# The second w_in converted during the attention, kept in device memory, and fetched later

## The chip, the cores and the metric

One core of one Trainium2 chip runs the kernel. The metric is the device time of an execution in microseconds, here as the median of three runs. The profile is of one execution.

## The reference, cut to what matters

Inputs come as float64 and are read as pairs of 32-bit words. Three stages follow each other: an attention over 2 batches, 8 heads, 768 rows and 64 columns, in which a query sees only keys of its own cluster; a layer pair with a SiLU; a layer pair with a PReLU. The change touches only how `moe2_w_in`, the first weight of the last pair, is brought in.

```python
def _moe_ref(x, w_in, w_out):
    h = x @ w_in
    g = h * (1.0 / (1.0 + np.exp(-h)))
    return (g @ w_out).astype(np.float32)

def _moe2_ref(x, w_in, w_out, alpha):
    h = x @ w_in
    g = np.maximum(h, 0.0) + alpha * np.minimum(h, 0.0)
    return (g @ w_out).astype(np.float32)

def reference(**kwargs):
    ...
    attn_out = _attn_ref(**attn_kwargs)
    x = np.ascontiguousarray(attn_out.transpose(0, 2, 1, 3)).reshape(B * S, H * D)
    x = _moe_ref(x=x, **moe_kwargs)
    return _moe2_ref(x=x, **moe2_kwargs)
```

Here x has 1536 rows of 512; w_in is 512 x 2048 and w_out 2048 x 512 in both pairs.

## The kernel before, in words

**Number format.** Each fp32 factor is kept as two fp16 parts (hi and lo) with a power of two as scale, and each product is three fp16 matmuls (hi hi, hi lo, lo hi). A weight is handled in eight pieces. A piece of 1 MB comes in as float64 (`load_piece`, L649), is made fp32 on the chip (`to_f32`: L660 on ACT, L664 on ACT or L668 on POOL, L671 and L674 on DVE), its sum of squares is taken (`sum_sq`, L700 on ACT, for the second pair), summed over the partitions by a matmul with ones (`all_sum`, L223 on PE), turned into a scale by small DVE instructions (`pow2_scale`, L172 to L179), and split into the two fp16 parts (`split`). `split` has four modes: in "a" and "d" DVE makes lo (L687, L682), in "b" and "c" POOL does (L693, L697); "c" also scales on POOL (L695) and makes hi on ACT (L696). The strings SPLIT and EXP_ON choose, piece by piece, the mode and the engine of the third step.

**Attention.** It works in units: one head of one tile of 128 queries, 96 units in all, 48 for each batch. A unit computes the scores (L509 and L513 on PE), their negated maximum (L517 on DVE), after every second unit the rows that carry the maxima (`to_rows`, L529 to L541), the scores again in the other orientation (L561, L562), the exponential (L564 on ACT), its hi part (L570 on ACT) and lo part (L571 on DVE), and the product with the values (L586 to L596 on PE). The maxima run two units ahead, the values two units behind. After four units a half of a tile of attention output is scaled and split (`x_done`, L613 to L623), and after eight units it is transposed by a DMA from SyncE's queue (L626).

**Layer 1** (first weight pair) takes the tiles in seven chunks and is interleaved with the attention: 32 steps a chunk, between which `attend` emits units up to UNITS_BY_CHUNK. A chunk has 192 matmuls of the first product (L951, with L959 to L965 on ACT and DVE behind them) and 192 of the second (L984, with L991 behind).

**Layer 2** (second weight pair) runs after that in three blocks of 512 rows: for each of 16 f twelve matmuls (L1056), then L1065 and L1066 on DVE, L1069 on ACT, L1070 on DVE; then the second product (L1087) and the output (L1093, L1095). Its input is split by `split_x2` (L1033 to L1043).

**The second weights.** `w2_start` (L1110) is called when the last unit has been emitted. It loads alpha (L1005, L1008) and hangs the tasks of both second weights into the list `bg`, from which one task is taken per step of layer 1: loads of w_in into three buffers of 8 KB a partition, `conv` and `scale` of its eight pieces, loads of w_out into the same three buffers, `conv` of its eight pieces, and its scale. The eight splits of w_out (`late`) follow in layer 2, two per f. They write into the place (o_w) of w_in of layer 1.

**What sets the order.** The Python order is a priority. A scheduler with a timing model of its own orders each engine's instructions before the run: it moves one ahead where it expects it to be ready. So work of later lines stands between that of earlier ones, and each engine then keeps to its list. DMAs go out from SyncE's list.

**Memory.** One arena holds everything; regions are used again when free. o_kvraw (8 KB a partition) takes raw K and V until the second batch is prepared; o_x2 takes the result of layer 1, its last 8 KB that of the last two chunks; w_in of layer 2 lies at o_a + 24 KB, where the attention has V, Q and o_kvraw.

## Time and profile before

| | |
|---|---|
| median of 3 runs | 877.53 us (876.75 to 878.41) |
| the profiled execution | 876.54 us |
| its span, first to last instruction | 874.6 us |
| mean granted TensorE clock | 0.963 of full speed |
| PE / DVE / ACT / POOL busy | 772.2 / 590.0 / 476.0 / 100.3 us |

The profile is of one execution, so sums over its rows are made against 876.54 us. "Busy" counts time in which an instruction is at work; a busy PE is not PE at its peak. "Idle before" is time that an engine stood before an instruction, with the instruction that ended it. Engines: PE is TensorE, DVE VectorE, ACT ScalarE, POOL GpSimd, SP SyncE with its queue.

### The profile page before, as it was taken

The page shows a single profiled execution, that of the slowest core. Times are in us where ns is not written, and L with a number is a line of the kernel's source. Part 1 is how long each engine was busy: PE and PEld are TensorE (multiplying, and loading weights), DVE is VectorE, ACT ScalarE, POOL GpSimd, SP SyncE. Part 2 cuts the span into 40 slices and gives each one's busy share as a digit, 9 for nine tenths or more (in the row PEclk, how much of TensorE's full clock was granted, in tenths as well). Part 3 has the DMA queues.
Part 4 walks back from the last instruction along what each step waited for, and adds up shares of the span by engine and source line. Part 5 has one row for each costly group of instructions (what it writes and reads, how often), then busy time and mean ns, then how long its engine had stood idle before and what let it go on. Part 6 is the DMA issues. An engine that isn't in the chain of part 4 may idle for free.

```text
span 874.6 us, 19047 instructions
## 1 busy us (share of the span) xinstructions
PE 772.2 (88%) x8196; PEld 570.1 (65%) x8196; DVE 590.0 (67%) x1253; ACT 476.0 (54%) x701; POOL 100.3 (11%) x126
## 2 busy tenths in 40 slices
PE   2475679799999999999999969989879999999998
PEld 1364469689988888877888857877334444444443
DVE  7898979968787477587867679496894058206700
ACT  7876848867677464565755696777631013102200
POOL 4400000000022220000000014431550000000000
PEclk9977589999999999999999989999999999999999
DMA  8969710422334341113103055445000000000000
GB/s 269 261 142 238 253 25 15 105 25 27 62 66 89 68 85 32 25 14 62 25 14 39 14 193 158 145 145 193 1 0 13 25 13 0 13 25 13 1 24 25
DMA packets 91077, 64.29 MB, mean 74 GB/s; under 512 B 66800, under 2 KB 77040, under 8 KB 90864
## 3 DMA queue, kind: packets, MB, share of 16 engines
q1 hardware_dynamic: 90992, 63.07, 27.8%
q8 instruction: 64, 1.05, 0.5%
q14 instruction: 21, 0.17, 0.1%
HBM read 44.08 MB, written 3.15 MB: 54 GB/s over the span
## 4 chain that ended last, share of the span: by engine, by line
PE 61%; DVE 16%; DMA 8%; ACT 6%; issue 2%; POOL 2%; DVEq 0%; POOLq 0%; SPq 0%; ACTq 0%
PE w L1087 9%; PE w L984 9%; PE w L951 8%; PE w L1056 8%; PE m L1087 5%; PE m L1056 4%; DMA arena<-arena 4%; DMA arena<-in_moe_w_in_dram 3%; PE s L509 3%; PE s L561 3%; PE s L562 3%; PE s L513 3%; DVE arena L674 2%; DVE arena L671 2%; DVE arena L687 2%
## 5 line engine op out<-in xcount | busy, mean ns | idle before, releaser
L984 PE MATMUL w<-arena 128*128 128x256 f16 (+1 forms) x1248 | 129.3, 256 | 5.2 <-DVE arena L687 3.0
L951 PE MATMUL w<-arena 128*128 128x256 f16 (+1 forms) x1200 | 126.2, 257 | 4.6 <-DVE arena L960 2.9
L564 ACT ACTIVATE arena<-s,stat 128x768 f32<-128x768 f32 x96 | 86.3, 899 | 79.1 <-PE s L562 78.4
L984 PEld LDWEIGHTS <-arena 128*128 128x128 f16 x1344 | 114.7, 98 | 20.6 <-issue 4.3
L951 PEld LDWEIGHTS <-arena 128*128 128x128 f16 x1344 | 115.3, 99 | 18.3 <-issue 3.6
L517 DVE TENSOR_REDUCE stat<-s 128x1 f32<-128x768 f32 x96 | 91.5, 954 | 38.4 <-PE s L513 37.2
L1056 PEld LDWEIGHTS <-arena 128*128 128x128 f16 x576 | 56.7, 99 | 76.3 <-issue 10.6
L1087 PEld LDWEIGHTS <-arena 128*128 128x128 f16 x576 | 56.4, 98 | 68.0
L571 DVE TENSOR_TENSOR arena<-arena 128x768 f16<-128x768 f32 x96 | 92.8, 967 | 8.0 <-ACT arena L570 7.9
L1056 PE MATMUL w<-arena 128*128 128x512 f16 x384 | 87.9, 383 | 7.2 <-DVE arena L1066 7.2
L1087 PE MATMUL w<-arena 128*128 128x512 f16 x384 | 84.0, 379 | 0.0
L561 PE MATMUL s<-arena 120*128 120x128 f16 x576 | 80.6, 225 | 3.8 <-ACT arena L541 2.8
L1069 ACT ACTIVATE arena<-arena,stat 128x512 f16<-128x512 f32 x48 | 34.6, 721 | 90.4 <-DVE arena L1066 88.5
L1065 DVE TENSOR_SCALAR arena<-w,stat 128x512 f32<-128x512 f32 x32 | 23.9, 748 | 87.2 <-PE w L1056 86.7
L570 ACT ACTIVATE arena<-arena 128x768 f16<-128x768 f32 x96 | 80.7, 841 | 1.9
L562 PE MATMUL s<-arena 128*128 128x128 f16 x576 | 80.5, 225 | 0.0
L509 PE MATMUL s<-arena 80*128 80x384 f16 x192 | 66.3, 345 | 13.0 <-DMA arena<-arena 12.8
L586 PE MATMUL x<-arena 128*128 128x65 f16 x576 | 73.4, 197 | 4.3 <-ACT arena L570 2.5
L592 PE MATMUL x<-arena 128*128 128x65 f16 x576 | 68.7, 197 | 8.5 <-DVE arena L571 8.4
L589 PE MATMUL x<-arena 128*128 128x64 f16 x576 | 73.2, 198 | 0.0
L513 PE MATMUL s<-arena 128*128 128x384 f16 x192 | 66.6, 347 | 0.0
L592 PEld LDWEIGHTS <-arena 128*128 128x128 f16 x576 | 55.8, 101 | 11.4 <-DVE arena L571 9.7
(169 smaller groups left out, 1431.8 us busy)
## 6 DMA issues: line engine op xcount, KB each, us to landing
arena<-in_moe_w_in_dram SPq DMA_DIRECT2D x16, 1024.0 KB, 5.8
arena<-in_moe_w_out_dram SPq DMA_DIRECT2D x16, 1024.0 KB, 5.5
arena<-in_k_dram SPq DMA_DIRECT2D x8, 384.0 KB, 4.1
arena<-in_q_dram SPq DMA_DIRECT2D x6, 512.0 KB, 4.6
arena<-in_v_dram SPq DMA_DIRECT2D x8, 384.0 KB, 5.5
out_dram<-arena SPq DMA_DIRECT2D x12, 256.0 KB, 2.0
arena<-in_moe_alpha_dram SPq DMA_DIRECT2D x1, 1024.0 KB, 4.8
arena<-arena SPq DMA_TRANSPOSE x53, 3.6
```

The lines of the kernel that those rows point to most:

```text
L509: nc.tensor.matmul(out=out, lhsT=qt2[0:D + C], rhs=kt2[0:D + C, j * th:(j + 1) * th], start=True, stop=False,)
L513: nc.tensor.matmul(out=out, lhsT=qt1, rhs=kt1[:, j * th:(j + 1) * th], start=False, stop=True,)
L517: nc.vector.tensor_reduce(out=un_cols[:, c:c + 1], in_=sc[:, :, :S // 2], axis=AX.XY, op=ALU.max, negate=True)
L561: nc.tensor.matmul(out=out, lhsT=kt2[0:k, t], rhs=qt2[0:k], start=True, stop=False)
L562: nc.tensor.matmul(out=out, lhsT=kt1[:, t], rhs=qt1, start=False, stop=True)
L564: nc.scalar.activation(out=view(o, F32, 2, S // 2), in_=sc[:, :, :S // 2], func=ACTF.Exp, scale=d[:, pr:pr + 1],)
L571: nc.vector.tensor_tensor(out=pt[:, 1], in0=p, in1=pt[:, 0], op=ALU.subtract)
L592: nc.tensor.matmul(out=out, lhsT=pt[:, T + t], rhs=vt[:, t, 0:D + 1], start=False, stop=False)
L951: nc.tensor.matmul(out=hp[:, r], lhsT=wi[:, a, kd, r * 128:r * 128 + 128], rhs=mov(bb, kd), start=(i == 0), stop=(i == 3 * KD - 1),)
L984: nc.tensor.matmul(out=acc, lhsT=wo[:, a, f % 2, dt * 128:(dt + 1) * 128], rhs=g[:, f, bb], start=(i == 0), stop=(i == 3 * KF - 1),)
L1056: nc.tensor.matmul(out=hp, lhsT=in_piece(o_a + 24 * KB, f // 2)[:, a, kd, f % 2 * 128:][:, :128], rhs=x[bb][:, kd], start=(i == 0), stop=( ...
L1087: nc.tensor.matmul(out=acc, lhsT=g[:, f, a, t * 128:(t + 1) * 128], rhs=out_piece(o_w, f // 2)[:, bb, f % 2], start=(i == 0), stop=(i == 3 ...
```

## The change

The tasks of the second w_in leave `w2_start`. `in_tasks` gets an argument `via`, two places of 4 KB a partition: a piece is split into one of them and stored from there to a tensor in device memory (`kept`). The attention calls these steps itself: at unit 51 the first load, from unit 53 on every five units a `conv`, and two units after it the `scale`, which also splits, stores and issues the next load. There is one raw buffer, o_kvraw, and the two places lie in the last 8 KB of o_x2. All eight pieces use split mode "c" and POOL for the third step of `to_f32`. In `w2_start` eight DMAs (`fetch`) bring the parts to o_a + 24 KB; they stand in `bg` behind the three loads of w_out and ahead of its conversions. The sums of the second w_in use the PSUM bank "m" in place of "s".

```diff
+W2_IN_AT = 51
+W2_IN_STEP = 5
...
-SPLIT = ("aaaaaaaa", "aaaaaaaa", "dbdbdbdb", "dccdcbbc")
-EXP_ON = ("aaaaaaaa", "aaaaaaaa", "appppapp", "papapppp")
+SPLIT = ("aaaaaaaa", "aaaaaaaa", "cccccccc", "dccdcbbc")
+EXP_ON = ("aaaaaaaa", "aaaaaaaa", "pppppppp", "papapppp")
...
+    dram_p = ctx.enter_context(tc.tile_pool(name="dram", bufs=1, space=bass.MemoryType.DRAM))
...
-    def in_tasks(w, raws, o_dst, kind, modes, mp):
+    def in_tasks(w, raws, o_dst, kind, modes, mp, via=None):
...
+        if via:
+            kept = [
+                dram_p.tile([128, 2 * PC], F16, tag=f"kept{j}", name=f"kept{j}") for j in range(NPC)
+            ]
...
-            d = in_piece(o_dst, j)
+            d = in_piece(via[j % len(via)], 0) if via else in_piece(o_dst, j)
             t = raw(j)[:, :, 1].bitcast(F32).rearrange("p (a f) -> p a f", a=KD)
             split(t, d[:, 0], d[:, 1], m.s[:, j:j + 1], modes[j])
             load(j + len(raws))
+            if via:
+                nc.sync.dma_start(out=kept[j], in_=view(via[j % len(via)], F16, 2 * PC))
...
+        def fetch(j):
+            nc.sync.dma_start(out=view(o_dst + 4 * KB * j, F16, 2 * PC), in_=kept[j])
...
+            if u == W2_IN_AT:
+                assert ("v", B - 1, NP - 1) in did and ("k", B - 1, NP - 1) in did
+                w2["in"] = in_tasks(
+                    w2_in, [o_kvraw], o_a + 24 * KB, "m", SPLIT[2], EXP_ON[2],
+                    [o_x2 + 16 * KB, o_x2 + 20 * KB],
+                )
+                w2["in"].loads[0]()
+            j, i = divmod(u - W2_IN_AT - 2, W2_IN_STEP)
+            if 0 <= j < NPC:
+                if i == 0:
+                    w2["in"].convs[j]()
+                elif i == 2:
+                    w2["in"].scales[j]()
...
-        w2["in"] = in_tasks(w2_in, raws, o_a + 24 * KB, "s", SPLIT[2], EXP_ON[2])
         w2["out"] = out_tasks(w2_out, raws, o_ts, o_w, w2["in"], "s", SPLIT[3], EXP_ON[3])
         bg.extend(
-            w2["in"].loads + w2["in"].tasks + w2["out"].loads + w2["out"].tasks
-            + [w2["out"].scale]
+            w2["out"].loads + w2["in"].fetches + w2["out"].tasks + [w2["out"].scale]
         )
```

The rest of the diff names the steps of `in_tasks` singly and asks for `via`, `kind` or `"out" in w2` where the code before asked whether `w2` was empty.

## Rows read from the trace of the kernel before

**Rows 1.** The page, part 1: busy time, share of the span and instructions.

```profile
PE 772.2 (88%) x8196; PEld 570.1 (65%) x8196; DVE 590.0 (67%) x1253; ACT 476.0 (54%) x701; POOL 100.3 (11%) x126
```

**Rows 2.** Windows: length, busy us (x instructions) of each engine, PEclk, DMA share, GB/s.

```profile
240.00:280.00 40.00, 37.70 (x515) 32.88 (x513) 35.67 (x87) 30.04 (x48) 9.35 (x11) 1.00 0.38 81
345.00:490.00 145.00, 141.44 (x1966) 123.66 (x1964) 103.65 (x244) 87.19 (x126) 0.00 (x0) 0.99 0.18 27
...
380.00:400.00 20.00, 16.44 (x245) 13.43 (x244) 15.88 (x39) 12.91 (x18) 0.00 (x0) 0.92 0.28 50
...
500.00:535.00 35.00, 24.32 (x299) 20.39 (x298) 29.52 (x51) 30.23 (x50) 6.46 (x4) 0.90 0.40 134
535.00:612.00 77.00, 70.30 (x624) 60.51 (x622) 53.54 (x76) 55.06 (x81) 24.99 (x16) 1.00 0.50 176
612.00:650.00 38.00, 29.98 (x137) 13.55 (x135) 34.94 (x47) 20.68 (x29) 25.67 (x13) 0.96 0.00 1
650.00:874.00 224.00, 220.79 (x1028) 100.41 (x1025) 83.36 (x127) 38.84 (x55) 0.00 (x0) 1.00 0.04 15
```

**Rows 3.** Waits of PE, 500 to 650: us in total, times, longest us.

```profile
PE w L1056 <- DVE arena L1066: 7.2, 4, 3.9
PE x L592 <- DVE arena L571: 5.1, 2, 4.9
PE s L223 <- ACT arena L700: 3.9, 5, 1.5
```

**Rows 4.** Timeline of SyncE's queue: start us, us, the DMA issued.

```profile
396.96 2.62 SPq L626 DMA_TRANSPOSE arena<-arena  x1
...
504.42 0.37 SPq L649 DMA_DIRECT2D arena<-in_moe_w_in_dram  x1
...
535.17 1.24 SPq L626 DMA_TRANSPOSE arena<-arena  x1
...
559.16 46.94 SPq L649 DMA_DIRECT2D arena<-in_moe_w_out_dram  x8
```

**Rows 5.** DVE's groups by line and shape, 612 to 650: xcount | busy, mean ns.

```profile
L1070 DVE SCALAR_TENSOR_TENSOR arena<-arena,stat 128x512 f16<-128x512 f32 x9 | 11.9, 1323 | 1.4 <-ACT arena L1069 1.3
L1065 DVE TENSOR_SCALAR arena<-w,stat 128x512 f32<-128x512 f32 x7 | 5.2, 740 | 0.0
```

**Rows 6.** Groups of all engines, 490 to 680: xcount | busy, mean ns | idle before.

```profile
L674 DVE SCALAR_TENSOR_TENSOR arena<-arena 128x1024 int32<-128x1024 int32 x16 | 20.9, 1306 | 0.2
L671 DVE SCALAR_TENSOR_TENSOR arena<-arena 128x1024 int32<-128x1024 int32 x16 | 19.5, 1221 | 23.7 <-POOL arena L668 12.1 <-ACT arena L664 11.6
...
L668 POOL TENSOR_SCALAR arena<-arena 128x1024 f32<-128x1024 f32 x12 | 18.8, 1567 | 228.3 <-DMA arena<-in_moe_w_in_dram 201.0 <-ACT arena L991 15.1 <-DMA arena<-in_moe_w_out_dram 10.8
...
L700 ACT ACTIVATE arena<-arena 128x1024 f32<-128x1024 f32 x16 | 18.5, 1157 | 7.9 <-DVE arena L674 7.9
L660 ACT ACTIVATE arena<-arena 128x1024 int32<-128x1024 uint32 x16 | 18.5, 1154 | 13.3 <-DMA arena<-in_moe_w_in_dram 9.3 <-DMA arena<-in_moe_w_out_dram 4.0
...
L697 POOL TENSOR_TENSOR arena<-arena 128x1024 f16<-128x1024 f32 x4 | 10.2, 2572 | 0.0
...
L695 POOL TENSOR_SCALAR arena<-arena,stat 128x1024 f32<-128x1024 f32 x4 | 6.4, 1600 | 0.0
...
L696 ACT ACTIVATE arena<-arena 128x1024 f16<-128x1024 f32 x4 | 4.1, 1045 | 0.0
...
L176 DVE TENSOR_SCALAR stat<-stat 128x1 int32<-128x1 int32 x11 | 1.6, 144 | 0.1
```

**Rows 7.** The page, part 6: DMA issues, KB each, us to landing.

```profile
arena<-in_moe_w_in_dram SPq DMA_DIRECT2D x16, 1024.0 KB, 5.8
...
out_dram<-arena SPq DMA_DIRECT2D x12, 256.0 KB, 2.0
```

**Rows 8.** DVE's groups by line and shape, 345 to 490, as rows 5.

```profile
L571 DVE TENSOR_TENSOR arena<-arena 128x768 f16<-128x768 f32 x36 | 34.2, 951 | 4.0 <-ACT arena L570 3.9
```

More of the change, by code (lines that the diff above doesn't have):

```diff
@@ L730, in conv @@
             to_f32(raw(j), t, mp[j])
-            if w2:
+            if via:
                 sum_sq(t, junk, ss[:, j:j + 1])
@@ L736, in scale @@
         def scale(j):
-            if not w2:
+            if not via:
                 for o in range(4 * j, 4 * j + 4):
@@ L745, in scale @@
             load(j + len(raws))
+            if via:
+                nc.sync.dma_start(out=kept[j], in_=view(via[j % len(via)], F16, 2 * PC))
             if j == NPC - 1:
@@ L748, in scale @@
                 nc.vector.tensor_reduce(out=m.inv_smin, in_=m.inv, axis=AX.X, op=ALU.max)
+        def fetch(j):
+            nc.sync.dma_start(out=view(o_dst + 4 * KB * j, F16, 2 * PC), in_=kept[j])
         m.loads = [lambda j=j: load(j) for j in range(len(raws))]
+        m.fetches = [lambda j=j: fetch(j) for j in range(NPC)]
+        m.convs = [lambda j=j: conv(j) for j in range(NPC)]
         m.scales = [lambda j=j: scale(j) for j in range(NPC)]
@@ L773, in conv @@
         def conv(j):
-            if not w2 and j < 6:
+            if kind == "w" and j < 6:
                 for o in range(4 * j, 4 * j + 4):
@@ L778, in conv @@
             to_f32(raw(j), t, mp[j])
-            if w2:
+            if kind != "w":
                 sum_sq(t, raw(j)[:, :, 0].bitcast(F32), ss[:, j:j + 1])
@@ L1141, in cluster_attention_silu_prelu @@
             attend(first + (target - first) * (i + 1) // steps)
-            if done[0] >= NU + LAG and not w2:
+            if done[0] >= NU + LAG and "out" not in w2:
                 w2_start()
-            if w2:
+            if "out" in w2:
                 run_bg(W2_TASKS)
```

## The prediction, made before the changed kernel was run

> **What bounds the kernel now.** I read the page first: a span of 874.6 us in which PE is busy 772.2 us [rows 1]. A change that adds and removes almost no matmul can only pay by the 102 us in which PE stands still, so I asked the windows view where those lie. From 345 to 490 us, where units 51 to about 90 of the attention run between the two matmuls of layer 1, PE is busy 141.44 of 145 us; the 3.56 us that are missing all lie between 380 and 400. DVE is there at 103.65 us (71%), ACT at 87.19 (60%), and POOL does nothing at all [rows 2]. So this stage is bound by PE, and it has room elsewhere. From 500 us on that turns round: PE is idle 10.68 us of 500 to 535, 6.70 of 535 to 612 and 8.02 of 612 to 650, 25.4 us together, and 3.2 us in all that follows [rows 2].
>
> The list of PE's waits in 500 to 650 says what ends them [rows 3]: 7.2 us for L1066 of layer 2, 5.1 us for L571 of the last attention units, and 3.9 us for L700, the sum of squares that the summing matmul (L223) waits for. The SyncE timeline gives the order of events [rows 4]: the first w_in load at 504.42, the last transpose of attention output at 535.17, the first w_out load only at 559.16, since it needs a buffer that a w_in piece must have left. From that late start follows the late end of the w_out conversion, whose eight splits then fall into the first units of layer 2: POOL is busy 25.67 us of 612 to 650 [rows 2] and L1070 takes 1323 ns in the mean there [rows 5].
>
> **The change, part by part.** *Removed from the tail:* eight w_in conversions and splits. *Kept there:* eight w_out conversions and splits, now with the three raw buffers from the start, so that the first w_out load can go out where the first w_in load did, 559.16 - 504.42 = 55 us earlier [rows 4]. I go through the three stretches.
> - 612 to 650: the splits need the scale, and the place of w_in of layer 1, which the last L951 leaves. With conversions 50 us earlier both are there before layer 2 begins, so the splits run beside the last L984, where DVE, ACT and POOL have lost their w_in work. Of 8.02 us of idle I leave 1. What is late next is only DVE's own work per f, beside which PE is busy 220.79 of 224 us from 650 on [rows 2].
> - 535 to 612: the eight sums that PE waited for are gone from here (one sum over the w_out pieces stays). Of 6.70 I leave 2.
> - 500 to 535: w_out conversions take the place of the w_in ones beside the last units (the same ACT, POOL and DVE instructions), without the scales and splits. Of 10.68 I leave 7; the ends are 4 and 10.68.
>
> Gain: 25.4 - 10 = 15.4 us; with all ends 6 to 20.
>
> *Added to 345 to 490.* By the groups of instructions [rows 6] a piece costs DVE 1.22 + 1.31 + three scale instructions of 0.15 = 2.97 us, eight pieces 23.8; ACT 1.15 + 1.16 + 1.05 = 3.36 us, together 26.9; POOL 1.57 + 1.60 + 2.57 = 5.74 us, together 46. ACT would stand at 114 of 145 us, which is room. PE gets eight small sums, which are moved and not new. For DVE there is a second cost: beside POOL, its instructions with two operands in the arena become longer. L1070 takes 1323 ns while POOL is at work, against 740 ns for L1065, which handles the same 512 elements there [rows 5]; nine of them lost 9 x 0.58 = 5.2 us beside 25.67 us of POOL, 0.2 us for each us of POOL. With L571 and the conversion's own two passes as the instructions hit, I take 0.25: 46 x 0.25 = 11.5 us. DVE: 103.65 + 23.8 + 11.5 = 139 of 145 us, 96%.
>
> What does a PE stage lose beside such a DVE? The trace has one like it: 240 to 280, where K and V of the second batch are prepared with POOL: DVE 35.67 of 40 (89%), POOL 9.35, PE idle 2.30 us, 5.75% [rows 2]. For 96% I take 8%: 11.6 us of 145, less the 3.56 that are idle already: a loss of 8 us. The lower end is 0, since outside 380 to 400 PE did not stop at all with DVE at 71%; the upper end, with every us of POOL stopping DVE, is 103.65 + 23.8 + 46 = 173 us, 28 us more than the stage has. I stay by the row of 240 to 280, as it has the same mixture of engines.
>
> The Trainium skill's page "SBUF — State Buffer", section "Who interferes with whom", has a rule that speaks against this change: a VectorE instruction with two SBUF inputs and a GpSimd instruction that reads SBUF share a port pair under an exclusive lock, and the later one waits for the whole of the other. The trace agrees in kind (1323 against 740 ns), but 0.2 us per us says that most of POOL's time finds DVE in other work; taken at its fullest the rule gives the upper end of 28 us.
>
> The loss also has a place. Between 380 and 400 PE lacks layer 1 work: the tile that ends a chunk is transposed at 396.96 [rows 4], and any delay of units 53 to 65 widens that gap at once. Pieces 0 to 2 fall there. About 3 of my 8 us stand here.
>
> *Waits that the change adds.* One raw buffer serves all pieces, so a piece is a chain: load 5.8 us [rows 7], then 1.15 + 1.57 + 1.22 + 1.31 + 1.16 + 0.45 + 1.60 + 1.05 + 2.57, in all 17.9 us; the next comes five units later, and 36 units take 145 us [rows 8], 4.0 us each, so every 20.1 us. It fits with 2 us over. If it slips, ACT stands at L660 for the load with an L564 behind it, and PE behind that; in the tail ACT has already stood 9.3 us before L660 for w_in loads [rows 6]. Half of that would be within the 8 us. On SyncE's queue each store waits for POOL's last subtraction, and the transposes of q and of the attention output stand behind it; they are issued ahead of use by more than a piece's slip, apart from the one at 396.96. A store of 512 KB lies between the 2.0 us of a 256 KB output and the 5.8 us of a 1024 KB load [rows 7]; nobody waits for it. The eight fetches are 16 to 46 us by the same two rows, and the w_out loads 8 x 5.8 = 46 us at most; they have from the last transpose at 535 to the stretch of layer 2 at 612, and layer 2 takes its pieces one after the other, so I cost them at nothing. Were that cover gone, the first fetch would cost PE its 2 to 5.8 us once.
>
> **Sum.** 15.4 - 8 = 7.4 us of gain. The profiled execution took 876.54 us, 1.9 us more than its span; 876.54 - 7.4 = 869.1. Its time is 1.0 us under the median of the three runs (877.53), so for the median I say 870.0.
>
> **The rivals.**
> - *DVE becomes the bound of the attention stage (slower).* Place: L571, L671 and L674 between units 53 and 90; mechanism: POOL's 46 us stop DVE more than 0.25 us each. It decides where 103.65 + 23.8 + 46r exceeds 145 by the gain of 15.4, at r = 0.72. With r = 1 the stage is 28 us longer, and the time 877.5 + 28 - 15.4 = 890. The two-input rule on that page, taken at its fullest, is this case. For it: L571 stands in every unit, and POOL goes from 0 to 32% of the stage. Against it: the 0.2 measured beside layer 2, and PE's only 5.75% loss at 240 to 280. Chance 0.20.
> - *The room swallows the work.* ACT and DVE have 58 and 41 us free, PE's static order has slack of some units; the loss is 1 us, the time 877.5 - 14.4 = 863. For it: PE's idle time of 345 to 490 is all at 380 to 400. Against: the gap at 380 to 400, and 96% on DVE. Chance 0.20.
> - *The tail does not clear (about no change).* The scheduler places conversions by its own clock and may put the w_out ones just as thick beside the last units, or leave the splits behind layer 2's start, so that the change doesn't do what it says for the end: only the 4.7 us at 535 to 612 and 3 of 10.68 are won, 7.7 against a loss of 8: 878. For it: both kinds have the same raw buffers and the same line of instructions. Against: 55 us of earlier start. Chance 0.12.
> - *The forecast*, 0.48.
>
> **How the numbers follow.** A difference of 0.2% (1.8 us) is about what a measurement of this kernel can tell from none. Faster: nearly all of the forecast (0.45), the swallowed case (0.20), a quarter of the third (0.03): 0.68. Same: 0.03 of the forecast and 0.05 of the third, 0.08. Slower: the first rival and the rest of the third, 0.24. The range takes in the swallowed case with the fuller gain of 20 us (877.5 - 20 + 1 = 858) and reaches up into the first rival to 885, where r is 0.88: 103.65 + 23.8 + 46 x 0.88 is 7.5 more than 145 + 15.4. Beyond lie some 0.1 above and 0.05 below.
>
> **What would show it.** Each step is right if: POOL is busy 40 to 50 us in 345 to 490; PE is idle there for 8 to 15 us, 6 or more of it around 380 to 400; the first w_out load stands near 504; L1070 takes near 740 ns at the start of layer 2, and PE's wait for L1066 is gone; L223 waits for L700 in the attention and hardly in the tail. It is wrong if: L571's mean far above 1.2 us with DVE over 97% busy in the attention (first rival); splits on POOL beside L1056 still (third rival); ACT waiting at L660 for w_in loads more than 10 us in all, which would make the one raw buffer the cause; a fetch that L1056 waits for.

## The result, and the profile after

The changed kernel takes 886.48 us (median of four runs) against 877.14 us for the kernel before, measured beside it: ratio 1.0106, 95% interval 1.0074 to 1.0138. It is slower by 1.1%, where 870.0 was forecast; it also lies just above the range.

| | before | changed |
|---|---|---|
| span of the profiled execution, us | 874.6 | 885.7 |
| PE busy, us | 772.2 | 781.6 |
| span less PE busy, us | 102.4 | 104.1 |
| mean granted clock | 0.963 | 0.952 |
| first matmul of layer 2 (L1056 before, L1087 after), us | 609.7 | 631.2 |
| from there to the end, us | 264.9 | 254.5 |

The page of the changed kernel, part 1, answers to [rows 1]:

```profile
PE 781.6 (88%) x8196; PEld 577.4 (65%) x8196; DVE 584.4 (66%) x1249; ACT 473.6 (53%) x699; POOL 107.7 (12%) x136
```

PE's idle time hardly changed; it is busy 9.4 us longer with the same 8196 matmuls. Busy time multiplied by the granted clock is nearly the same in both (743.6 and 744.1 us), so the 9.4 us are the same work at a lower clock.

The windows of the changed kernel, columns as in [rows 2]. The last three are cut at its own start of layer 2:

```profile
345.00:490.00 145.00, 132.75 (x1741) 113.36 (x1740) 112.17 (x246) 95.75 (x136) 26.90 (x18) 0.95 0.37 91
...
380.00:400.00 20.00, 16.27 (x207) 12.61 (x205) 15.27 (x34) 13.69 (x20) 4.45 (x3) 0.83 0.32 93
400.00:420.00 20.00, 14.73 (x202) 12.23 (x200) 15.59 (x41) 11.12 (x17) 3.37 (x3) 0.83 0.55 123
...
520.00:540.00 20.00, 15.83 (x227) 13.38 (x227) 12.88 (x30) 14.72 (x23) 5.08 (x4) 0.83 0.47 154
540.00:560.00 20.00, 13.26 (x124) 10.78 (x122) 15.84 (x25) 16.80 (x30) 0.71 (x2) 0.83 1.08 396
...
612.00:631.00 19.00, 17.54 (x162) 15.80 (x162) 6.24 (x12) 6.67 (x14) 0.86 (x1) 1.00 0.00 1
631.00:655.00 24.00, 24.00 (x118) 11.33 (x115) 15.90 (x24) 6.97 (x11) 0.00 (x0) 1.00 0.00 1
655.00:885.00 230.00, 226.60 (x1056) 103.29 (x1056) 88.58 (x139) 42.03 (x60) 0.00 (x0) 1.00 0.04 14
```

Two things are to be seen. From 631 on the tail is clear: PE is full in the first 24 us of layer 2 and POOL does nothing, where it was busy 25.67 us before [rows 2]. And in 345 to 490 PE did 1741 matmuls in place of 1966 [rows 2], though no engine is full: DVE stands at 77%, ACT at 66%. At 141.44/1966 = 72 ns apiece, the mean of the kernel before, the 225 missing matmuls are some 16.2 us of work; 8.7 us of that are more idle time (12.25 for 3.56), and the other 7.5 us go to slower matmuls and to a different mixture of them. Much of the idle time and of the low clock lies in the same slices: 0.83 at 380 to 420, where 9.0 of the 12.25 us of idle are, and again at 520 to 560. Of the two levels, 1.2 and 2.4 GHz, 0.83 is about a third of the slice at the lower.

The groups of DVE in 345 to 490, columns as in [rows 5], answer to [rows 8]:

```profile
L576 DVE TENSOR_TENSOR arena<-arena 128x768 f16<-128x768 f32 x31 | 31.2, 1008 | 4.2 <-ACT arena L575 4.1
```

31 units pass in place of 36; the attention is five units, about 20 us, behind at 490. SyncE's timeline of the changed kernel, columns as in [rows 4], shows the same by its last transposes of attention output (L631):

```profile
407.59 1.24 SPq L631 DMA_TRANSPOSE arena<-arena  x1
...
515.23 0.37 SPq L654 DMA_DIRECT2D arena<-in_moe_w_in_dram  x1
523.88 1.25 SPq L631 DMA_TRANSPOSE arena<-arena  x1
...
533.57 0.38 SPq L654 DMA_DIRECT2D arena<-in_moe_w_out_dram  x1
...
550.28 6.67 SPq L631 DMA_TRANSPOSE arena<-arena  x1
557.05 16.11 SPq L654 DMA_DIRECT2D arena<-in_moe_w_out_dram  x4
```

The transpose of 396.96 [rows 4] comes at 407.59, the last one at 550.28 for 535.17. Layer 2 begins 21.5 us later and runs 10.4 us shorter: 11.1 us in all, the difference of the spans.

What the delay looks like from near is in DVE's timeline of the changed kernel, one lap of the attention at the end of a tile (start us, us, instruction, idle time before it and its releaser):

```profile
398.96 1.23 DVE L676 SCALAR_TENSOR_TENSOR arena<-arena 128x1024 int32<-128x1024 int32 x1
...
400.23 0.95 DVE L522 TENSOR_REDUCE stat<-s 128x1 f32<-128x768 f32 x1
401.09 0.15 DVE L618 TENSOR_SCALAR stat<-x 128x4 f32<-128x4 f32 x1
401.16 1.21 DVE L679 SCALAR_TENSOR_TENSOR arena<-arena 128x1024 int32<-128x1024 int32 x1
...
404.38 0.92 DVE L522 TENSOR_REDUCE stat<-s 128x1 f32<-128x768 f32 x1
405.23 0.95 DVE L576 TENSOR_TENSOR arena<-arena 128x768 f16<-128x768 f32 x1
406.09 0.15 DVE L535 SCALAR_TENSOR_TENSOR arena<-stat,arena 128x2 f16<-128x2 f32 x1
...
408.63 0.16 DVE L177 TENSOR_SCALAR stat<-m 128x1 int32<-128x1 int32 x1 [1.07 <-PE m L228]
...
411.22 0.96 DVE L522 TENSOR_REDUCE stat<-s 128x1 f32<-128x768 f32 x1 [2.17 <-PE s L518]
```

From 398.96 to 407.6 DVE has no gap; two passes of the conversion (1.23 and 1.21 us) stand in this list ahead of the small L535 at 406.09, which ends the rows that PE's L544 needs. PE's waits in 345 to 530 (us in total, times, longest) show who waited for it:

```profile
PE m L544 <- DVE arena L535: 5.6, 3, 4.3
PE s L566 <- ACT arena L546: 3.6, 6, 1.5
PE m L482 <- DMA arena<-arena: 2.6, 2, 2.0
PE x L597 <- DVE arena L576: 2.3, 4, 1.2
```

The 4.3 us are this lap. The kernel before has the same wait at the same tile (L539 for L530 at 394.93), its only one of that kind in 345 to 490, but it is 2.2 us long:

```profile
PE m L539 <- DVE arena L530: 2.2, 1, 2.2
```

So the two passes, 2.4 us together, come on top of a wait that was there. When the lap ends, ACT has waited 2.7 us for PE (L546), and DVE, full until then, next waits for PE (2.17 us). A mean of 77% over 145 us hides such laps.

### The profile page after: what moved, and what is told of

Its sections match the earlier page's. It is cut to its first block, busy times and chain, and to the rows that moved or that the text cites. A ratio compares the mean times of both kernels' runs of the same rounds, so it can differ in the third digit from the quotient of the medians.

```text
span 885.7 us, 19110 instructions
## 1 busy us (share of the span) xinstructions
PE 781.6 (88%) x8196; PEld 577.4 (65%) x8196; DVE 584.4 (66%) x1249; ACT 473.6 (53%) x699; POOL 107.7 (12%) x136
## 4 chain that ended last, share of the span: by engine, by line
PE 64%; DVE 14%; DMA 11%; ACT 6%; POOL 2%; issue 2%; SPq 0%; POOLq 0%; ACTq 0%; DVEq 0%
PE w L1015 11%; PE w L1087 9%; PE w L1118 9%; PE w L982 7%; DMA arena<-in_moe_w_in_dram 5%; PE m L1118 5%; PE m L1087 5%; DMA arena<-arena 5%; PE s L566 3%; PE s L567 2%; PE s L514 2%; PE s L518 2%; DVE stat L522 2%; DVE arena L676 2%; DVE arena L576 2%; DMA arena<-in_moe_w_out_dram 2%
## 5 line engine op out<-in xcount | busy, mean ns | idle before, releaser
L1015 PE MATMUL w<-arena 128*128 128x256 f16 (+1 forms) x1248 | 132.3, 259 | 4.9 <-DVE arena L692 2.6
L982 PE MATMUL w<-arena 128*128 128x256 f16 (+1 forms) x1200 | 126.1, 258 | 6.8 <-DVE arena L991 4.6
L982 PEld LDWEIGHTS <-arena 128*128 128x128 f16 x1344 | 116.0, 99 | 22.6 <-issue 7.9
L1015 PEld LDWEIGHTS <-arena 128*128 128x128 f16 x1344 | 116.1, 99 | 19.3 <-DVE arena L692 3.3
L576 DVE TENSOR_TENSOR arena<-arena 128x768 f16<-128x768 f32 x96 | 94.0, 980 | 10.9 <-ACT arena L575 10.7
L1118 PEld LDWEIGHTS <-arena 128*128 128x128 f16 x576 | 56.3, 98 | 68.0
L1087 PEld LDWEIGHTS <-arena 128*128 128x128 f16 x576 | 56.4, 98 | 67.2
L566 PE MATMUL s<-arena 120*128 120x128 f16 x576 | 83.4, 230 | 8.0 <-ACT arena L546 6.0
L1087 PE MATMUL w<-arena 128*128 128x512 f16 x384 | 86.0, 379 | 0.0
L1100 ACT ACTIVATE arena<-arena,stat 128x512 f16<-128x512 f32 x48 | 34.7, 722 | 95.4 <-DVE arena L1097 93.5
L1118 PE MATMUL w<-arena 128*128 128x512 f16 x384 | 84.0, 379 | 0.0
L567 PE MATMUL s<-arena 128*128 128x128 f16 x576 | 83.6, 230 | 0.0
L514 PE MATMUL s<-arena 80*128 80x384 f16 x192 | 66.8, 348 | 16.0 <-DMA arena<-arena 14.1
L591 PE MATMUL x<-arena 128*128 128x65 f16 x576 | 75.7, 199 | 4.5 <-ACT arena L575 2.7
L597 PE MATMUL x<-arena 128*128 128x65 f16 x576 | 70.4, 198 | 7.2 <-DVE arena L576 7.2
L594 PE MATMUL x<-arena 128*128 128x64 f16 x576 | 75.5, 199 | 0.0
L567 PEld LDWEIGHTS <-arena 128*128 128x128 f16 x576 | 59.6, 104 | 11.3 <-issue 10.7
```

The lines of the kernel that those rows point to most:

```text
L514: nc.tensor.matmul(out=out, lhsT=qt2[0:D + C], rhs=kt2[0:D + C, j * th:(j + 1) * th], start=True, stop=False,)
L566: nc.tensor.matmul(out=out, lhsT=kt2[0:k, t], rhs=qt2[0:k], start=True, stop=False)
L567: nc.tensor.matmul(out=out, lhsT=kt1[:, t], rhs=qt1, start=False, stop=True)
L576: nc.vector.tensor_tensor(out=pt[:, 1], in0=p, in1=pt[:, 0], op=ALU.subtract)
L982: nc.tensor.matmul(out=hp[:, r], lhsT=wi[:, a, kd, r * 128:r * 128 + 128], rhs=mov(bb, kd), start=(i == 0), stop=(i == 3 * KD - 1),)
L1015: nc.tensor.matmul(out=acc, lhsT=wo[:, a, f % 2, dt * 128:(dt + 1) * 128], rhs=g[:, f, bb], start=(i == 0), stop=(i == 3 * KF - 1),)
```

## The experiments

The first question was which half of the prediction fell, the gain or the cost; the next, what the cost consists of: load on an engine, POOL's lock, the DMAs and their queue, the place of the gap at 380 to 400, waits in the lists, or the hops of a piece from engine to engine. The table has all runs; "idle" is span less PE busy, "matmuls" those of 345 to 490 by the windows view, and kernels marked * leave out part of the work of the w_in pieces.

| kernel | ratio to before (95%) | span | PE busy | idle | matmuls |
|---|---|---|---|---|---|
| changed | 1.0106 (1.0074 to 1.0138) | 885.7 | 781.6 | 104.1 | 1741 |
| tail_alone * | 0.9821 (0.9791 to 0.9851) | 857.6 | 767.6 | 90.0 | 1969 |
| cost_alone | 1.0345 (1.0319 to 1.0372) | 904.5 | 786.2 | 118.3 | 1739 |
| late_start | 1.0312 (1.0275 to 1.0348) | 899.8 | 786.2 | 113.6 | 1709 |
| no_dma * | 0.9983 (0.9962 to 1.0005) | 868.8 | 773.4 | 95.4 | 1801 |
| tail_loads * | 0.9903 (0.9871 to 0.9935) | 862.4 | 770.5 | 91.9 | 1920 |
| loads_held * | 0.9769 (0.9741 to 0.9798) | 854.3 | 769.5 | 84.8 | 1969 |
| no_pool * | 0.9983 (0.9963 to 1.0003) | 873.6 | 774.1 | 99.5 | 1783 |
| act_only * | 0.9836 (0.9808 to 0.9865) | 857.1 | 767.8 | 89.3 | 1963 |
| dve_only * | 0.9846 (0.9814 to 0.9878) | 862.7 | 773.3 | 89.4 | 1917 |
| paced * | 0.9927 (0.9906 to 0.9949) | 866.2 | 775.4 | 90.8 | 1871 |
| scale_next | 1.0099 (1.0060 to 1.0138) | 881.0 | 777.0 | 104.0 | 1734 |
| spaced | 1.0091 (1.0063 to 1.0119) | 881.1 | 777.9 | 103.2 | 1739 |
| pool_queue | 1.0152 (1.0131 to 1.0172) | 887.6 | 782.9 | 104.7 | 1714 |
| half | 1.0051 (1.0034 to 1.0067) | 877.0 | 775.9 | 101.1 | 1874 |
| quarter | 1.0095 (1.0065 to 1.0125) | 883.0 | 778.4 | 104.6 | 1899 |
| early_free | 1.0046 (1.0021 to 1.0070) | 876.4 | 778.2 | 98.2 | 1737 |
| two_engines | 1.0052 (1.0028 to 1.0077) | 876.4 | 777.0 | 99.4 | 1755 |
| both_held | 1.0099 (1.0066 to 1.0131) | 885.0 | 780.0 | 105.0 | 1681 |

**The two halves.** tail_alone has no loads and no arithmetic for the pieces of w_in (zeros are stored and fetched); cost_alone converts w_in in the attention and once more in the tail as before.

```diff
 # tail_alone
-                w2["in"].loads[0]()
...
-                    w2["in"].convs[j]()
...
-                    w2["in"].scales[j]()
+                    w2["in"].stores[j]()
 # cost_alone, in w2_start: the second in_tasks writes w_in in the tail again
-            w2["out"].loads + w2["in"].fetches + w2["out"].tasks + [w2["out"].scale]
+            w2["in"].loads + w2["in"].tasks + w2["out"].loads + w2["out"].tasks
+            + [w2["out"].scale]
```

> The changed kernel without any load, conversion, sum or split of the second w_in: zeros are stored eight times at the units where the pieces were, and fetched at the end. What is left is the change's effect on the tail. Theory A (the tail gains what was forecast, about 15 us, and the arithmetic inside the attention costs more than that): 877 - 14 = 863, between 859 and 867. Theory B (the tail itself gives little, because eight fetches and the w_out loads crowd the last transposes): 872 or more.

> The attention as in the changed kernel, with loads, conversions, splits and stores, but the tail as in the kernel before: the second w_in is converted a second time there, and nothing is fetched. What is left is the cost inside the attention. Theory A: the units fall behind by about 20 us, some of which the layer 1 work covers: 877 + 20 = 897, between 890 and 902. Theory B: 884 or less.

The tail's gain is 875.53 - 860.04 = 15.5 us, as forecast (15.4). The cost with the tail of before is 906.01 - 875.53 = 30.5 us, and the changed kernel against tail_alone pays 26 to 28 (886.48 - 860.04 = 26.4; the spans differ by 28.1). So the gain stands and the 8 us of cost are wrong. The windows of tail_alone:

```profile
345.00:490.00 145.00, 140.56 (x1969) 122.93 (x1968) 104.52 (x245) 87.17 (x129) 0.15 (x1) 1.00 0.21 47
490.00:530.00 40.00, 29.18 (x405) 24.70 (x404) 30.02 (x55) 32.54 (x52) 2.79 (x2) 0.95 0.60 214
530.00:600.00 70.00, 70.00 (x633) 62.39 (x631) 39.83 (x54) 42.44 (x66) 25.18 (x16) 0.98 0.21 68
```

**The place.** If the gap at 380 to 400 decides, the pieces belong behind it.

```diff
 # late_start
-W2_IN_AT = 51
-W2_IN_STEP = 5
+W2_IN_AT = 64
+W2_IN_STEP = 3
```

> The changed kernel with the first load at unit 64 and a piece every three units in place of unit 51 and every five, so that no piece falls in front of the tile that chunk 4 of layer 1 waits for. Theory A with the cost spread over all units: 884 to 890, as eight pieces now crowd 24 units. Theory D (the cost is the gap before that chunk, where PE has no layer 1 work): about 10 us less than the changed kernel, 876 or less.

It rises to 901.85. The stretch 400 to 420 is indeed full (PE 20.00 of 20), but in 490 to 600 PE stands idle for 24.5 us, at a clock of 0.84, as its windows show:

```profile
345.00:490.00 145.00, 128.91 (x1709) 110.75 (x1707) 106.80 (x231) 87.19 (x124) 19.61 (x13) 0.97 0.27 67
490.00:600.00 110.00, 85.49 (x895) 70.37 (x895) 77.48 (x131) 73.83 (x110) 23.80 (x17) 0.84 0.56 182
```

So the cost does not go when that gap is spared. The pieces were also denser here, so the run does not tell the place alone.

**The DMAs.** no_dma loads, stores and fetches one piece only, and all eight conversions work on that one buffer; tail_loads adds the eight loads to tail_alone; loads_held does so too, with each load and store issued behind the last transpose on SyncE; pool_queue is the changed kernel with the loads and stores on GpSimd's queue.

```diff
 # no_dma
-            load(j + len(raws))
-            if via:
+            if not via:
+                load(j + len(raws))
+            if via and j == 0:
 # loads_held (tail_loads: the same without issue_after)
+            if j + 1 < NPC:
+                issue_after(load(j + 1), tr[0])
+            issue_after(nc.sync.dma_start(out=kept[j], in_=view(via[j % len(via)], F16, 2 * PC)), tr[0])
 # pool_queue
-                return load_piece(w[:, j * FW:(j + 1) * FW], raw(j))
+                return load_piece(w[:, j * FW:(j + 1) * FW], raw(j), nc.gpsimd if via else None)
...
-                nc.sync.dma_start(out=kept[j], in_=view(via[j % len(via)], F16, 2 * PC))
+                nc.gpsimd.dma_start(out=kept[j], in_=view(via[j % len(via)], F16, 2 * PC))
```

> The changed kernel with one w_in load and one store in place of eight: the same arithmetic eight times on the same buffer, and eight fetches of one stored piece. Theory A (the arithmetic in the lists of ACT and DVE delays the units): 883 to 887, as the changed kernel. Theory C (1 MB loads and 512 KB stores delay the transposes of q and of the attention output, which share the queue): 876 or less. Between, both take part.

> The tail alone (zeros stored and fetched, no arithmetic on the second w_in) plus the eight 1 MB loads at the units where the pieces were split. Theory C (loads and stores crowd the transposes on the shared queue): the 12 us between the changed kernel and the one without DMAs appear here too, 860 + 12 = 872, at least 868. Theory E (the DMAs cost because ACT stands in front of the conversion until the load is there, with the exponentials behind it): nothing waits for these loads, so 859 to 864.

> The tail alone plus the eight loads and eight stores, each held in SyncE's queue behind the last transpose of its unit, so that they are spread as in the changed kernel; no arithmetic on the second w_in. Theory C2 (the DMA engines are taken from the transposes): 868 to 873, as the crowded loads gave 868. Theory W (DMAs cost through the waits of the steps that need them): 860 to 863.

> The changed kernel with the eight loads and eight stores issued from POOL's queue in place of SyncE's. Theory C1 (the transposes are late because they stand behind these DMAs in SyncE's queue): most of the 12 us goes, 874 to 879. Theory C2 (they are late because the DMA engines themselves are taken): 884 to 889. Theory E (the loads come too late for ACT): no change either, or slower by what POOL needs to issue them.

Without the DMAs 12 of the 26 us are gone, 14.6 stay. tail_loads cost 8 us more than tail_alone, but its loads had nothing to wait for and were issued in a bunch, all eight within 325 to 367 us, so it doesn't speak of the changed kernel. Spread over 343 to 471 us in loads_held they cost nothing: 856.01 is the fastest kernel of the study, and its attention runs like that of before, beside 113 GB/s. It is even 4 us under tail_alone, which does less, so an order held by hand may be worth something by itself (the two intervals just overlap):

```profile
345.00:490.00 145.00, 141.44 (x1969) 123.66 (x1967) 103.63 (x245) 87.39 (x126) 0.00 (x0) 0.99 0.44 113
```

The other queue gives 888.59, the same as the changed kernel or a little worse (POOL spends 8.3 us of 345 to 490 on issuing these DMAs, which may hide a small gain). So neither the traffic nor the queue makes the cost by itself; what the loads cost in the changed kernel they cost together with the steps that wait for them.

**Engine by engine.** In no_pool, which goes on from no_dma, POOL's three steps of a piece are left out; paced is that with ACT's and DVE's steps held at their units; act_only and dve_only have only the three steps of ACT, or the two passes of DVE, besides the small sums and scale instructions, which both keep. POOL's steps alone were not run.

```diff
 # paced (act_only: without DVE's passes; dve_only: without ACT's steps)
+        if keep:
+            issue_after(i, last["a"])
...
+        if keep:
+            issue_after(i, last["d"])
```

> The kernel without DMAs of the pieces, and also without POOL's three steps of a piece, so that only ACT's and DVE's steps stand between the units (the lo parts are zeros). Theory A (what ACT and DVE have in their lists delays the units): 871 to 876, near the 874.7 of the kernel without DMAs. Theory P (POOL: DVE blocked beside it, DVE and ACT waiting for its results): half or more of the 14.6 us over the tail alone goes, 867 or less.

> The kernel without DMAs of the pieces and without POOL's steps, but with each piece's steps on ACT and DVE held by issue order behind the exponential and the subtraction of the unit where they belong (without POOL and loads the scheduler had moved all eight pieces to the first 60 us). Theory A (ACT's and DVE's own steps cost): 870 to 876. Theory P (POOL's part costs, and only the crowding hid it): near the tail alone, 860 to 866.

> As the paced kernel, without DVE's two long passes of a piece: ACT's three steps (26.9 us together), the sums on PE and the small scale instructions stay. Tail alone is 860.0. If both engines' lists cost by the length of what is put into them, ACT has 27 of 51 us and the time is 867 to 869; if ACT alone carries the cost, 871 or more; if DVE alone, 863 or less.

> As the paced kernel, without ACT's three steps of a piece: DVE's two long passes, the sums on PE and the small scale instructions stay. If both lists cost by length: 866 to 868. If DVE alone carries the cost: 870 or more. If ACT alone, 863 or less.

no_pool can't be read: with nothing to wait for, its pieces were placed in a bunch at 328 to 394 us. The three paced kernels can. ACT's steps alone leave the time 1.2 us above tail_alone, DVE's 3.0, both together 8.3; with POOL's steps, by no_dma, 14.6, and with the DMAs 26.4. (By the ratios, which take out the small drift of the kernel before: 0.15, 0.25, 1.06, 1.62 and 2.85%; the interval of tail_alone alone is 0.3% to each side, so the first two are not told from nothing.) ACT at 106.69 of 145 us costs nothing, and DVE at 116.81 little:

```profile
345.00:490.00 145.00, 139.88 (x1963) 122.48 (x1962) 104.70 (x264) 106.69 (x153) 0.00 (x0) 1.00 0.17 31
```

```profile
345.00:490.00 145.00, 139.39 (x1917) 121.01 (x1916) 116.81 (x276) 84.72 (x123) 0.00 (x0) 0.98 0.15 27
```

These are the windows of act_only and of dve_only. Both engines are busier there than in the changed kernel (95.75 and 112.17), which does 180 to 220 matmuls fewer. The load on one of these two engines is not the cause, and what was run alone, ACT's steps, DVE's steps and the DMAs, sums to far less than the 26.4 us of the whole. (no_dma's steps are not held at their units as those of paced, so its step from 8.3 to 14.6 is not POOL's alone.)

**Waits in the lists.** Within 345 to 530 the steps of the pieces wait 19.4 us in the lists of ACT and DVE of the changed kernel; the largest of them, by its waits view:

```profile
ACT arena L665 <- DMA arena<-in_moe_w_in_dram: 7.9, 5, 2.7
...
ACT arena L705 <- DVE arena L679: 4.6, 3, 1.8
```

scale_next splits a piece one unit earlier; spaced holds each step behind a step of a unit by which its input should be there; early_free gives the fp32 piece a place of its own, so that the raw buffer is free earlier.

```diff
 # scale_next
-                elif i == 2:
+                elif i == 1:
 # spaced
+            if part:
+                issue_after(i, last["hi"])
...
+            if part:
+                issue_after(i, last["max"])
 # early_free
+                t, junk = view(via[0], F32, PC), view(via[1], F32, PC)
...
+                load(j + 1)
```

> The changed kernel with the split one unit after the conversion in place of two, so that the next load goes out a unit (about 4.5 us) earlier before its conversion. Theory E (waits for loads in ACT's list): most of the 7.9 us that ACT stood in front of L665 for loads go, and the time falls to 880 or less. Theory C: no fewer DMAs and the same contention, 884 to 889.

> The changed kernel, all work and all DMAs, but each step of a piece stands in its engine's list behind a unit's step that comes after its input: L665 behind the hi part (L575) of its unit, DVE's passes behind the next unit's maximum, the sum of squares behind that unit's L575, the split's hi part behind L575 of the unit after. Theory W (the waits of a piece's steps in ACT's and DVE's lists, 19 us in the changed kernel, hold up the units behind them): those waits fall below 10 us and the time to 878 or less. Theory L (the steps cost by their own length, or by the DMAs, wherever they stand): 884 to 889.

> The fp32 piece gets a place of its own, so that the raw buffer is free after DVE's second pass and the next load starts some two units earlier; the same instructions otherwise. If ACT's waits for loads (L665, 7.9 us within 345 to 530 in the changed kernel, none in the kernel without the loads) and what stands behind them in ACT's list make the 12 us between the changed kernel and the one without the pieces' DMAs, L665 waits for a DMA by under 2 us and the time is 874 to 879. If the loss is the coupling of a piece's steps across engines whatever they wait for, or contention of the DMAs with the unit's transposes, the wait goes and the time stays at 883 to 889.

The first two did not do what they were made for: in scale_next ACT's wait for loads rose to 12.7 us, at 884.34; in spaced all such waits fell only to 15.9 us, at 884.95. In early_free each load does go out earlier, by 16 to 31 us from the second piece on: the fourth piece's stands at 391.21, where the changed kernel has its third (390.37) and its fourth only at 414.11; the last stands at 484.45 for 515.23. But the conversion's first steps moved ahead with the loads, so ACT still stands in front of L665, and DVE's second pass must now wait until POOL has read the fp32 place of the piece before. SyncE's timeline (the fourth and the fifth load) and ACT's and DVE's waits of early_free:

```profile
391.21 0.37 SPq L654 DMA_DIRECT2D arena<-in_moe_w_in_dram  x1
...
413.21 0.37 SPq L654 DMA_DIRECT2D arena<-in_moe_w_in_dram  x1
```

```profile
ACT arena L665 <- DMA arena<-in_moe_w_in_dram: 13.5, 7, 2.7
...
DVE arena L676 <- POOL arena L673: 13.2, 7, 3.1
```

Yet it takes 879.6, 7 us less (5 by the ratios), with more waits (13.5 for 7.9 us, 13.2 for 6.3). So the sum of these waits does not set the cost either. Up to 490 the two are level (1737 and 1741 matmuls); the difference comes behind it, where early_free's PE is full from 490 to 520 and the changed kernel's is idle for 4.6 us. Its pieces are done earlier: its last store stands at 521.74 for 534.05, its first w_out load at 523.44 for 533.57.

How a piece holds the units can be read in the critical view of the changed kernel, the chain of work that ended last, followed back at each step to what released it or to the instruction before it on its engine (start us, us, what):

```profile
367.30 1.13 ACT arena L701
...
368.50 2.14 POOL arena L702
370.66 5.83 DMA arena<-in_moe_w_in_dram
...
376.65 1.17 POOL arena L673
377.84 1.23 DVE arena L676
379.07 0.46 DVE stat L522
...
379.85 1.22 DVE arena L679
381.07 0.88 DVE arena L576
...
381.99 0.20 PE x L597
```

The split of one piece (L701, L702) frees the raw buffer, the next load fills it, POOL and DVE convert what it brought, and the unit's L576 stands behind L679 in DVE's list, with PE's L597 behind it. In the kernel before the chain of the same stretch, 363 to 382, is PE's matmuls alone. In 345 to 560 the chain of the changed kernel passes three loads of w_in pieces (370.66, 436.02 and 515.23), 17.3 us together.

**Fewer hops, fewer pieces.** two_engines takes POOL out of a piece's chain (ACT and DVE do its steps); both_held is that with early_free's edit and, as a third, the loads and stores held behind the transposes; half and quarter convert four or two pieces in the attention and the rest in the tail.

```diff
 # two_engines: SPLIT[2] and EXP_ON[2]
-"cccccccc"  "pppppppp"
+"aaaaaaaa"  "aaaaaaaa"
 # half (quarter: 67, 12, 2)
-W2_IN_AT = 51
-W2_IN_STEP = 5
+W2_IN_AT = 51
+W2_IN_STEP = 10
+NVIA = 4
```

> GpSimd's three steps of a piece are done by ScalarE and VectorE (modes a in place of c and p): the chain of a piece has three handoffs to GpSimd fewer, but ACT gets two steps more of some 1.1 us each and DVE one, about 2 and 1 us a piece, 18 and 9 us over the attention. If it is the number of handoffs between ordered lists that costs (GpSimd's steps were worth 6.3 us between the kernel with ACT and DVE alone and the one without DMAs), the time falls to 878 to 883 in spite of the load. If what costs is the work in ACT's and DVE's lists, whose shares in 345 to 490 would go from 66 and 77 % to about 75 and 82 %, it rises to 888 to 896.

> Both edits together, and each load and store issued behind the last transpose on SyncE, as in the kernel whose loads alone cost nothing. The version that should beat the kernel before if waits for loads, handoffs and crowded transposes are each a part of the cost: 866 to 873. If the cost is in the presence of the steps on ACT and DVE themselves, it is no faster than the better of the other two, 878 to 890.

> Four pieces in the attention, one every ten units, and four converted in the tail ahead of the w_out loads. If cost and gain are both linear in the pieces: half of the 9 to 11 us that the change lost, 880 to 883. If the cost grows faster than the pieces (a delay of the units costs only what the layer 1 work at hand does not cover): 874 or less, which would beat both kernels. If the tail's gain needs all eight pieces out of it: 884 or more.

> Two pieces in the attention, at units 69 and 81, past the gap before chunk 4, and six in the tail ahead of the w_out loads. By the line through the kernel before (no piece), half (plus 5 us for four) and the changed kernel (plus 10 for eight): 877 to 878. If the first pieces out of the tail are worth most, as w_out can start one round of buffers earlier, and two pieces are covered by layer 1: 872 or less, which beats both kernels.

Three hops fewer win 6 us (880.46; 5 by the ratios) although ACT has more to do (101.32 of 145 us); POOL is then idle all through the stretch, so no lock between POOL and DVE makes the 20 us that this kernel still pays over tail_alone. The two edits that won 7 and 6 us alone win 2 with the third (884.75; under 0.1% by the ratios), with the fewest matmuls of all by 490 (1681); whether the two alone would add was not run. Nor is the cost in proportion to the pieces: half comes to 880.36 and quarter to 885.1, as the pieces that stay in the tail cost there again (in 490 to 600 PE is idle for 27 us in quarter, for 16.8 in the kernel before):

```profile
345.00:490.00 145.00, 139.09 (x1899) 120.71 (x1897) 106.32 (x245) 87.22 (x126) 8.23 (x5) 0.99 0.20 38
490.00:600.00 110.00, 82.99 (x871) 68.84 (x868) 80.59 (x127) 80.52 (x117) 26.63 (x16) 0.90 0.51 163
```

No kernel with the whole computation beat the kernel before.

## Why the prediction was wrong

**Right.** *The gain*: 15.5 us measured, 15.4 forecast. Its parts were less exact, so that the sum is met to 0.1 us is luck: from layer 2's start on 264.9 - 254.2 = 10.7 us are won in tail_alone, 8.0 of them idle time (7 forecast for 612 to 650) and 2.7 slower matmuls, before it 609.7 - 603.4 = 6.3 (8.4 forecast). In the changed kernel PE's wait for L1066 is gone, and L1101 (L1070 before) takes 744 ns in 631 to 670, near the 740 named as its length without POOL [rows 5]:

```profile
L1101 DVE SCALAR_TENSOR_TENSOR arena<-arena,stat 128x512 f16<-128x512 f32 x12 | 8.9, 744 | 1.0 <-ACT arena L1100 1.0
```

*PE's idle time in 345 to 490*: 12.25 us against the 11.6 that came out of the row of 240 to 280. This is luck too: the 11.6 were read for a DVE at 96%, and it stood at 77%. *Fetch and store*: no wait of layer 2 for a fetch, though by the page, part 6, a store took 6.7 us to land and a fetch 9.0, more than the 2.0 to 5.8 us that the prediction read [rows 7].

**Wrong: "a loss of 8 us".** The step that failed is the one from there to the loss, "11.6 us of 145, less the 3.56 that are idle already". It took idle time for lost work, and the stretch for the whole of the damage.
- The clock had no term. In the same 145 us PE did some 16.2 us less work, not 8.7, as it also ran at 0.95 of its clock for 0.99. Against act_only, which has the same 8196 matmuls, the changed kernel's profiled execution is 28.6 us longer: 14.8 us of idle time and 13.8 us of slower matmuls. In the four slices above that stand at 0.83, PE also had gaps of 3.7 to 6.7 us in 20.
- The delay went on behind 490. The last transpose of attention output comes 15.1 us later than before and 19.7 us later than in tail_alone (530.6), and the first w_out load, expected "near 504", at 533.57 (506.45 in tail_alone). Layer 2 starts 631.2 - 603.4 = 27.8 us later than in tail_alone, which is the cost.
- "It fits with 2 us over" did not hold. The loads of the pieces stand 18.5 to 45.3 us apart, 27 in the mean, where the chain of a piece was to come every 20.1. ACT stood 9.4 us before L665 for them in 320 to 540, just under the 10 that the prediction named as the sign of the one raw buffer, and early_free, where that buffer is free earlier, is the faster by 7 us.
- The transposes had no term apart from the one at 396.96. In 345 to 530 PE waited 4.3 us for them (2.6 at L482, 1.7 at L514), and in the kernel before not at all; their three lines landed in 4.9, 4.1 and 4.7 us (medians) for 3.1, 3.1 and 3.0.

**Wrong: DVE's share as the measure.** "103.65 + 23.8 + 11.5 = 139 of 145 us, 96%" came to 112.17, 77%. DVE got less to do in the stretch as the units came later, five fewer, and the pieces too: six of the eight. A share is an outcome of the waits as much as a cause; the lap at 399 to 408 shows DVE full for 9 us and then waiting for the engine that had waited for it.

**Wrong in size: POOL's time, not its price.** POOL's steps took 1.15, 1.20 and 2.14 us in the attention, not the 1.57, 1.60 and 2.57 read beside the crowded tail [rows 6], and six pieces passed in the stretch: 26.90 us in place of 46. What DVE lost for each of them was sized about right. In 345 to 490 L576 takes 1008 ns against 951 [rows 8], L996 801 against 685, and four short instructions of the units 208 to 666 against 156 to 221 (L534, L535, L558, L620). With their counts that is 9.0 us, 0.33 us for each us of POOL where I took 0.25. In two_engines, with POOL idle, all six are back within 5 ns of the kernel before. The loss comes in whole instructions: four of the six L702 in the stretch made one short DVE instruction end with them. Here L620, 0.15 us in the median, starts 0.03 us after L702:

```profile
479.90 2.13 POOL L702 TENSOR_TENSOR arena<-arena 128x1024 f16<-128x1024 f32 x1 [1.26 <-ACT arena L701]
479.93 2.13 DVE L620 TENSOR_TENSOR stat<-stat 128x4 f32<-128x4 f32 x1
```

This is the rule of the Trainium skill's page "SBUF — State Buffer", section "Who interferes with whom", as the prediction gives it. PE was seen to stop for it once in the stretch: L544 waited 0.93 us at 390.41 for an L535 that L702 had made 1.00 us long. So the first rival, though it gave 890, was not what happened: its rate had to be 0.72, and DVE was never near its bound over the stretch. The second (all swallowed) fell with the 26 us over tail_alone, the third (tail does not clear) with the gain.

**What the cost is.** Shown: ACT's steps alone (1.2 us), DVE's alone (3.0), the traffic by itself (loads_held) and the sum of the pieces' waits (early_free) do not make it, another queue does not take it away (pool_queue), and without POOL in the stretch 20 us stay (two_engines). It grows with the chain: 8.3 us for ACT's and DVE's steps together, 14.6 with POOL's, 26.4 with the DMAs. The trace shows a way for this: the steps of a piece, which follow each other over load, ACT, POOL, DVE, PE and back, stand in lists that the units also go through in order, and the chain that ended last runs through a load, L673, L676 and L679 before the unit's L576 and L597 get their turn. That such holds make all of the 26 us is inferred from what is left, not shown: spaced, made to shorten them, hardly did, and early_free and two_engines are faster with longer waits of the pieces. Two rivals stand. One is the plan: each edit lets the scheduler order all lists anew, and the time of the same computation moved between 880 and 902 us. The other is the one raw buffer, which puts the load on the chain; a second one was not tried. Nor was an order with the steps of pieces and units placed by hand, with the durations of the chip.

## What to carry to other kernels

Room on each engine (here 23% on DVE, 34% on ACT) does not say that a dependent chain over several engines can be laid into a tightly ordered loop: test it first one engine at a time and then together, and look whether the whole costs more than its parts, as here. Judge a stretch by the work done in it (matmuls or units per us) rather than by idle time, and give the clock its own term wherever a change opens gaps on TensorE. Where a change takes work from one place to another, run the removal alone first: it gives the most that can be won, here 15.5 us, against which every form of the addition can be held.

## What the hardware showed that was not expected

- About half of the loss against act_only shows as slower matmuls, and the granted clock goes with them: busy times 767.8 (act_only), 773.3 (dve_only), 775.4 (paced), 781.6 us (changed) for the same matmuls, with clocks 0.965, 0.958, 0.957 and 0.952; the product stays within 740.8 to 744.1. From act_only to paced the span grows by 9.1 us, of which 7.6 are busy time and 1.5 idle.
- Eight loads of 1 MB and eight stores of 512 KB cost nothing when each is issued behind a transpose and nothing waits for them (loads_held), with PE's work in 345 to 490 unchanged to three matmuls in 1966.
- GpSimd's steps ran at 1.15 to 2.14 us in the attention and 1.57 to 2.57 us in the tail of the kernel before: the same instructions differ by a fifth or more with the stretch they run in.
- A DVE instruction of 0.15 us can take 2.1 us beside one GpSimd instruction (L620 beside L702, above). The mean of a group of long instructions does not show that: L576 grew by 6% only, while most of the 9.0 us fell on short ones and on L996.
